# Infini-attention plus SiLU MLP on one core: k's first masked tile read from PSUM by two engines, the exponentials' table loaded ahead of the last v copy, the first tile of x in two halves, and a newly searched order of pieces

## The chip, the core and the metric

The kernel runs on one core of a Trainium2 chip. The metric is the device time of one execution in microseconds (us), the median of three runs. Engines are named as in the profile: PE is TensorE (matmuls), PEld its weight loads, DVE is VectorE, ACT is ScalarE, POOL is GpSimd, SP is SyncE, which here only issues DMAs (a q behind an engine's name means its DMA issues).

## The reference, cut to what matters

```
xn = layernorm(A_x)                       # 2048 rows of 512, bf16
q, k, v = xn @ wq, xn @ wk, xn @ wv       # 32 heads of 16, 4 segments of 512 rows
for s in 4 segments:
    p     = softmax(qs ks^T * 16**-0.5 + mask)      # within the segment
    a_dot = p @ vs
    a_mem = (phi(qs) @ M) / (phi(qs) . z + 1e-6)    # phi(t) = t+1 if t > 0 else exp(t)
    o     = g * a_mem + (1 - g) * a_dot             # g = sigmoid(beta), by head
    M += phi(ks)^T @ vs;  z += sum phi(ks)
out = A_x + o @ wo + silu(xn @ w1) @ w2             # w1 512 x 1792, w2 1792 x 512
```

The mask is added where the key's row lies behind the query's (`ar[:, None] < ar[None, :]`), so attention is causal within a segment.

## The kernel before, in words

All tensors are tiled to 128 partitions. x has 16 tiles of 128 rows; a segment is four of them. Four heads of k or q lie in 64 partitions, so one tile of kT or qT (128 partitions x 512 rows of a segment) holds eight heads, and a segment has four such tiles.

No scheduler orders the work. A string, ORDER, lists 1333 pieces by name, and the kernel issues them in that order (`tc.manual_schedule()`); each engine gets its instructions in the order of the list and waits, in place, for what an instruction needs. So the list is the queue of every engine at once. A piece's name holds its kind, its segment and its place. The ones that matter here:

- `xc`, `xd` (together `xs`): mean and variance of one tile of x on VectorE. `xq`, `xi`: square root on ScalarE, reciprocal on VectorE, for the first four tiles; `xg`: the same on GpSimd for four later tiles at once. `Nv`: the normalised tile. `X` with `Xa` or `Xv`: its transposes by TensorE and the copy to xnT by ScalarE or VectorE; `XD`: a DMA transpose, for the later tiles.
- `v`, `k`, `q`, `h`: parts of the products of xnT with wv, wk, wq, w1. In segments 0 and 1 a part is a quarter of a tile, in segments 2 and 3 a half. In segment 0, parts 0 and 1 of k, q and h cover the first 256 rows, parts 2 and 3 the others. `va` and `vv`, `qa` and `qv`, `ka` and `kv` copy the finished tile from PSUM, on ScalarE or on VectorE; `ha` is the tanh of a tile of h, `hv` the rest of its SiLU.
- `ka`/`kv` call `k_copy`: one copy of the tile to kT, and then two copies by GpSimd from kT to k3, with every odd or every even head set to zero (`pm_odd`, `pm_even`, which the piece `odd` makes). The score products need them, because a row group of TensorE spans two heads.
- `fp`, `fa`, `fv`: phi of k, its positive part on GpSimd, its exponential on ScalarE, the sum on VectorE (`gp`, `ga`, `gv` for q).
- `S` and a number: one score block. TensorE fills psS, a tile of four PSUM banks of which there is one, and ScalarE takes the exponential of all 2048 elements of a partition (line 707). There are 72. GpSimd then sets the masked corners to zero (line 718), in place and into a second tile, lows. `E` and `O` weigh v with them (line 763), for the even and the odd heads; `Ev`, `Ea`, `Ov`, `Oa` copy the result.
- `o`, `oc`, `od`, `oh`: whole, half, quarter and half-width products of the output; `st`, `sh` store. `n`, `z`, `d`, `r`, `R`, `w`, `W`, `s`: the memory's part and the softmax's division.
- `tb`: one small exponential on ScalarE, `first_exp` (line 304), in front of which the build puts the load of the table with exp and tanh. The square roots ahead of it use another table, which the small square root on line 185 loads.
- `busy`: products of zeros on TensorE, which fill its time before x is there.
- `kind`, `odd`, `omask`, `ones`, `zeros`: constants.

TensorE has three tilings: whole, four strips of columns (`cols`) and four of rows (`rows`, for scores). A dense product is issued whole or as four strips, by what stands before and behind it in the list.

The loads at the start: tiles 0 and 2 of x, then wv in halves, wk, wq, and the rest are issued by SyncE, tiles 1 and 3 by ScalarE (line 158 and on). The DMAs use eight semaphores in turn, so a ninth waits, in its issuing queue, until the one eight places ahead has landed. PSUM has four single banks for everything else than psS.

## Time and profile before

| what | value |
|---|---|
| median of three runs (lowest to highest) | 222.32 us (222.01 to 222.53) |
| profiled execution | 222.15 us |
| its span in the profile | 220.4 us |
| PE busy | 214.9 us, 97% |
| ACT busy | 184.0 us, 83% |
| DVE busy | 179.7 us, 82% |
| POOL busy | 135.1 us, 61% |
| granted TensorE clock, mean | 0.999 |

The span runs from the first to the last instruction of the profile; 1.75 us of the execution lie around it. Busy shares are means over a start, a long middle part and an end, whose limits differ. In the rows of the timeline stand start (us from the span's start), length (us), engine, line, operation, output and inputs, count, and in brackets the idle time before it with the releaser. Rows of several instructions are merged. In the rows by stretch stand, for each engine in the order PE, PEld, DVE, ACT, POOL, the busy time and the number of instructions, then the granted clock, the busy share of the DMA engines and GB/s.

### The profile page before, as it was taken

The page shows a single profiled execution, that of the slowest core. Times are in us where ns is not written, and L with a number is a line of the kernel's source. Part 1 is how long each engine was busy: PE and PEld are TensorE (multiplying, and loading weights), DVE is VectorE, ACT ScalarE, POOL GpSimd, SP SyncE. Part 2 cuts the span into 40 slices and gives each one's busy share as a digit, 9 for nine tenths or more (in the row PEclk, how much of TensorE's full clock was granted, in tenths as well). Part 3 has the DMA queues.
Part 4 walks back from the last instruction along what each step waited for, and adds up shares of the span by engine and source line. Part 5 has one row for each costly group of instructions (what it writes and reads, how often), then busy time and mean ns, then how long its engine had stood idle before and what let it go on. Part 6 is the DMA issues. An engine that isn't in the chain of part 4 may idle for free.

```text
span 220.4 us, 9441 instructions
## 1 busy us (share of the span) xinstructions
PE 214.9 (97%) x4057; PEld 117.2 (53%) x4057; DVE 179.7 (82%) x368; ACT 184.0 (83%) x173; POOL 135.1 (61%) x253
## 2 busy tenths in 40 slices
PE   7999999999999999999999999999999999999994
PEld 7666645655553444454544444455454544455662
DVE  7789999988889788776897888969789887579554
ACT  3699999999999999999998999999989997971000
POOL 6089667997769976876669696693756364320000
PEclk9999999999999999999999999999999999999999
DMA  5993549552014221223303130142242020232313
GB/s 183 373 385 87 74 27 304 106 77 58 21 28 122 88 59 29 50 51 76 102 17 95 40 96 4 28 92 59 52 120 64 15 76 7 75 94 68 109 51 97
DMA packets 32746, 19.61 MB, mean 89 GB/s; under 512 B 14656, under 2 KB 32192, under 8 KB 32704
## 3 DMA queue, kind: packets, MB, share of 16 engines
q1 hardware_dynamic: 30080, 16.39, 28.6%
q10 hardware_dynamic: 2624, 2.62, 3.9%
q8 instruction: 31, 0.51, 1.0%
q14 instruction: 11, 0.09, 0.2%
HBM read 9.96 MB, written 2.10 MB: 55 GB/s over the span
## 4 chain that ended last, share of the span: by engine, by line
PE 79%; ACT 10%; DVE 4%; POOL 4%; issue 2%; POOLq 0%
PE ps L331 21%; PE psO L333 16%; PE ps L333 13%; PE psS L701 10%; PE psO L331 9%; ACT Pb L707 7%; PE psV L763 6%; PE psS L333 4%; POOL Pb L718 2%; DVE xn_t L310 1%; POOL lows L718 1%; ACT ex L408 1%; ACT th L477 1%; PE psM L437 1%; DVE stats L281 1%
## 5 line engine op out<-in xcount | busy, mean ns | idle before, releaser
L707 ACT ACTIVATE Pb<-psS 128x2048 bf16<-128x2048 f32 x72 | 135.2, 1878 | 7.5 <-PE psS L701 6.4
L718 POOL TENSOR_SCALAR_AFFINE_SELECT Pb<-Pb 128x256 bf16<-128x256 bf16 (+2 forms) x120 | 66.1, 571 | 22.3 <-ACT Pb L707 19.5
L482 DVE SCALAR_TENSOR_TENSOR hT<-th,ps 128x512 bf16<-128x512 bf16 x56 | 37.7, 679 | 9.1 <-ACT th L477 8.5
L718 POOL TENSOR_SCALAR_AFFINE_SELECT lows<-Pb 64x256 bf16<-64x256 bf16 (+1 forms) x56 | 26.7, 490 | 27.7 <-ACT Pb L707 25.3
L333 PE MATMUL psO<-w_sb,hT 128*32 128x512 bf16 (+2 forms) x716 | 42.5, 319 | 0.0
L331 PE MATMUL ps<-xnT,w_sb 128*128 128x512 bf16 (+1 forms) x160 | 35.2, 334 | 0.0
L477 ACT ACTIVATE th<-ps 128x512 bf16<-128x512 f32 x56 | 33.0, 598 | 2.2 <-PE ps L333 2.1
L333 PEld LDWEIGHTS <-hT 128*32 128x32 bf16 x884 | 21.8, 96 | 14.0 <-issue 3.3
L333 PE MATMUL ps<-xnT,w_sb 128*32 128x512 bf16 (+1 forms) x480 | 27.1, 341 | 0.1
L701 PE MATMUL psS<-qT,k 32*128 32x64 bf16 (+3 forms) x512 | 23.0, 233 | 0.8 <-ACT Pb L707 0.3
L331 PE MATMUL psO<-w_sb,hT 128*128 128x512 bf16 (+2 forms) x87 | 22.7, 334 | 0.0
L701 PEld LDWEIGHTS <-k 32*128 32x128 bf16 x512 | 9.8, 92 | 23.2 <-issue 21.7
L763 PE MATMUL psV<-Pb,Vz 128*32 128x448 bf16 (+7 forms) x512 | 21.6, 286 | 0.3 <-POOL Pb L718 0.3
L331 PEld LDWEIGHTS <-w_sb 128*128 128x128 bf16 x160 | 14.9, 98 | 12.1 <-issue 1.6
L763 PEld LDWEIGHTS <-Vz 128*32 128x32 bf16 x768 | 16.5, 97 | 9.1 <-issue 1.1
L376 POOL TENSOR_SCALAR k<-kT,pm_odd 128x512 bf16<-128x512 bf16 x16 | 12.0, 748 | 8.0 <-ACT kT L373 7.0
L333 PEld LDWEIGHTS <-w_sb 128*32 128x32 bf16 x480 | 11.9, 96 | 7.3 <-issue 1.9
L331 PE MATMUL ps<-wv_sb,xnT 128*128 128x512 bf16 x56 | 15.1, 381 | 0.2
L701 PE MATMUL psS<-qT,kT 16*128 16x448 bf16 (+3 forms) x256 | 14.7, 269 | 0.0
L333 PE MATMUL psO<-wo_sb,oT 128*32 128x512 bf16 x156 | 14.4, 380 | 0.0
L331 PE MATMUL ps<-xnT,wk_sb 128*128 128x256 bf16 (+1 forms) x64 | 13.6, 326 | 0.0
L793 DVE CAST oraw<-psV 128x512 bf16<-128x512 f32 x16 | 11.0, 689 | 3.0 <-PE psV L763 2.9
(110 smaller groups left out, 321.2 us busy)
## 6 DMA issues: line engine op xcount, KB each, us to landing
spr<-rz SPq DMA_DIRECT2D x56, 64.0 KB
x_res<-in_A_x_dram SPq DMA_DIRECT2D x16, 128.0 KB
out_dram<-o_out SPq DMA_DIRECT2D x15, 128.0 KB
w_sb<-in_B_w_dram SPq DMA_DIRECT2D x1, 1792.0 KB
w_sb<-in_B_w_dram ACTq DMA_DIRECT2D x1, 1792.0 KB
x_hi<-in_A_x_dram SPq DMA_DIRECT2D x2, 512.0 KB
wv_sb<-in_A_wv_dram SPq DMA_DIRECT2D x2, 256.0 KB
wk_sb<-in_A_wk_dram SPq DMA_DIRECT2D x1, 512.0 KB
```

The costliest lines, as they stand in the source:

```text
L281: nc.vector.bn_stats(out=stats[t][:], in_=xs(t, t + 1)[:, 0, :])
L310: eng.tensor_scalar(out=xn[t][:], in0=xs(t, t + 1)[:, 0, :], scalar1=mv_all[:, t, 0:1], scalar2=rstd_all[:, t, 0:1], op0=ALU.subtract, op1 ...
L331: return [nc.tensor.matmul(out, lhsT=lhsT, rhs=rhs, start=start, stop=stop, skip_group_check=True)]
L333: nc.tensor.matmul(out[c : c + 32], lhsT=lhsT[:, c : c + 32], rhs=rhs, start=start, stop=stop, tile_position=(0, c), skip_group_check=True,)
L376: nc.gpsimd.tensor_scalar(out=to, in0=frm, scalar1=keep[:, 0:1], scalar2=1.0, op0=ALU.mult, op1=ALU.mult)
L477: nc.scalar.activation(out=th[:], in_=sts[s]["h", ft][:, :], func=AF.Tanh, scale=0.5)
L482: nc.vector.scalar_tensor_tensor(out=st["hT"][:, ft, :], in0=st.pop(("th", ft))[:], scalar=1.0, in1=st.pop(("h", ft))[:, :], op0=ALU.add, ...
L701: nc.tensor.matmul(psS[:, g, c : c + q2 - q1], lhsT=keys[rows], rhs=st["qT"][rows, dt, q1:q2], start=True, stop=True, tile_position=(32 * ...
L707: exp = nc.scalar.activation(out=Pb[:, :, :], in_=psS[:, :, :], func=AF.Exp, scale=SCALE)
L718: over[id(Pb)].append(nc.gpsimd.affine_select(out=out, in_=in_, compare_op=ALU.is_ge, fill=0.0, base=base, pattern=[[0, out.shape[1]], [1, ...
L763: nc.tensor.matmul(psV[32 * g : 32 * g + 32, q0 : q0 + nq], lhsT=Vzs[s % 2][:, kt, 4 * dt + g, par : par + 2, :].rearrange("p a d -> p (a ...
L793: copy(out=oraw[:], in_=sts[s].pop(("psV", 0))[:, :])
```

## The change

Tile 0 of x is loaded as two halves of 64 rows, one from each of the two queues; tiles 1, 2 and 3 follow on the same queues as before. A new piece, `kf`, is used for the first tile of k of segment 0: ScalarE copies the tile from PSUM to kT, VectorE makes the odd heads' masked copy straight from PSUM and ScalarE the even heads'. All other tiles of k are made as before. In the list, `tb` stands between the two v copies `va0.0` and `va0.1`, three pieces of constants stand later than the first statistics, the first `busy` has 40 products, and the pieces behind are in another order (of which the first lines are shown). The number of score blocks and of products is the same, but for the 40 products of zeros.

```diff
-kind odd omask ones0 ones1 zeros xc0 xd0 xc1 xq0 xi0 Nv0 busy44 xd1 xq1 xc2 xi1 X0.1 Nv1 xd2 Xa0.1 busy6 v0.0.0 v0.0.1 xq2 X1.1 Xa1.1 xs3 v0.0.2 v0.0.3 xq3 v0.1.0 xi2 v0.1.1 v0.1.2 v0.1.3 Nv2 xi3 X2.1 va0.0 va0.1 Nv3 Xv2.1 X3.1 Xv3.1 k0.0.0 k0.0.1 k0.1.0 k0.0.2 k0.0.3 k0.3.0 q0.0.0 q0.0.1 q0.0.2 q0.0.3 ka0.0 fp0.0 qv0.0 tb fa0.0 q0.2.0 k0.1.1 k0.1.2 k0.1.3 kv0.1 fp0.1
-S0 q0.1.0 q0.1.1 q0.1.2 q0.1.3 k0.3.1 xs4 xs6 xs7 xs5 xg4.4 q0.2.1 q0.2.2 qa0.1 q0.2.3 qv0.2
-S2 v0.2.0 v0.2.1 k0.3.2 k0.3.3 kv0.3 fa0.1 v0.3.0 v0.3.1 v0.3.2 Nv7 v0.2.2 XD7 v0.2.3
-S1 Nv5 vv0.2 h0.5.0 h0.10.0 h0.10.1 h0.10.2 v0.3.3 vv0.3 xs8 Nv6 XD6 h0.5.1 h0.5.2 XD5 h0.5.3 ha0.5
-S3 q0.3.0 q0.3.1 q0.3.2 q0.3.3 hv0.5 k0.2.0 qv0.3 Nv4 XD4 k0.2.1 k0.2.2 tanh h0.10.3 ha0.10
-S4 fv0.0 k0.2.3 kv0.2 h0.11.0 h0.11.1 h0.11.2 h0.11.3 ha0.11 fv0.1 v1.3.0 v1.3.1 v1.3.2 v1.3.3
-S7 vv1.3 hv0.10 h0.13.0 h0.13.1 fa0.3 h0.13.2 hv0.11 fp0.2 O0 E0 Ev0 Ov0
-S5 v1.2.0 v1.2.1 v1.2.2 h0.13.3 ha0.13 v1.2.3 xs9 vv1.2 q1.1.0 q1.1.1 q1.1.2 q1.1.3 qv1.1 xs11
-S11 Om0 v1.0.0 hv0.13 v1.1.0 v1.0.1 v1.0.2 v1.1.1 v1.0.3 h0.1.0 h0.1.1 h0.1.2 fp0.3 ga1.1
...
+ones0 ones1 zeros xc0 xd0 xc1 xq0 xi0 Nv0 busy40 xd1 xq1 xc2 xi1 X0.1 Nv1 xd2 Xa0.1 busy6 v0.0.0 v0.0.1 xq2 X1.1 Xa1.1 xs3 v0.0.2 v0.0.3 xq3 v0.1.0 xi2 v0.1.1 v0.1.2 v0.1.3 Nv2 va0.0 xi3 tb Nv3 X2.1 Xv2.1 X3.1 k0.0.0 k0.0.1 k0.1.0 Xv3.1 k0.0.2 k0.0.3 q0.0.0 q0.0.1 va0.1 odd kf0.0 xs6 q0.0.2 q0.0.3 qa0.0 xs4 k0.1.1 k0.1.2 k0.1.3 ka0.1
+S0 fa0.1 q0.1.0 q0.1.1 k0.3.0 q0.1.2 q0.1.3 xs5 qv0.1 xs7 q0.2.0 q0.2.1 q0.2.2 q0.2.3 qv0.2 xg4.4
+S2 k0.2.0 k0.2.1 k0.2.2 k0.2.3 v0.2.0 v0.2.1 k0.3.1 kv0.2 Nv5 XD5 fp0.1 k0.3.2 k0.3.3 Nv6 fa0.0
+S1 v0.2.2 h0.11.0 h0.11.1 h0.11.2 h0.11.3 ha0.11 v0.2.3 kv0.3 q0.3.0 q0.3.1 h0.13.0
+S3 h0.13.1 vv0.2 fv0.1 XD6 h0.13.2 h0.13.3 ha0.13 Nv7 q0.3.2 q0.3.3 qv0.3 v0.3.0 v0.3.1 v0.3.2 hv0.11 v0.3.3 vv0.3 XD7
+S4 h0.5.0 h0.5.1 h0.5.2 h0.5.3 ha0.5 v1.2.0 v1.2.1 v1.2.2 Nv4 fp0.0 hv0.13 v1.1.0 v1.1.1 XD4 xs9 fp0.2 hv0.5
+S7 h0.10.0 v1.1.2 v1.1.3 vv1.1 h0.10.1 h0.10.2 E0 v1.2.3 xs8 Ev0 fa0.2
+S5 h0.1.0 h0.1.1 h0.10.3 ha0.10 fv0.0 h0.1.2 h0.1.3 fp0.3 vv1.2 k1.2.0 k1.2.1 k1.2.2 k1.2.3
+S11 fv0.2 kv1.2 fp1.2 v1.0.0 v1.0.1 v1.0.2 v1.0.3 ha0.1 hv0.10 h0.7.0 h0.7.1 h0.7.2 vv1.0 h0.7.3 xs10 O0 Ov0 fa0.3
...
@@ -154,16 +154,18 @@
     wo_sb = cpool.tile([P, DT, D], BF16, name="wo_sb")
     beta_r = cpool.tile([P, 1], BF16, name="beta_r")
 
-    def load_x(eng, t0, n):
+    def load_x(eng, t0, n, rows=slice(0, P)):
         eng.dma_start(
-            out=xs(t0, t0 + n),
-            in_=x_flat[t0 * P : (t0 + n) * P, :].rearrange("(n p) d -> p n d", p=P),
-        )
-
-    load_x(nc.sync, 0, 1)
+            out=xs(t0, t0 + n)[rows],
+            in_=x_flat[t0 * P : (t0 + n) * P, :].rearrange("(n p) d -> p n d", p=P)[rows],
+        )
+
+    load_x(nc.sync, 0, 1, slice(0, P // 2))
+    load_x(nc.scalar, 0, 1, slice(P // 2, P))
     load_x(nc.scalar, 1, 1)
     load_x(nc.sync, 2, 1)
     load_x(nc.scalar, 3, 1)
+
     def load_w(eng, w_sb, W, k0, k1):
         eng.dma_start(out=w_sb[:, k0:k1, :], in_=W.rearrange("(ko ki) n -> ki ko n", ki=P)[:, k0:k1, :])
 
@@ -367,15 +369,28 @@
 
 
 
-    def k_copy(s, dt, copy=nc.vector.tensor_copy):
+    def k_tiles(s, dt):
         kT = seg_tile(s, "kT")
         k3 = sts[s]["k3", dt] = segp.tile([P, TPS, 3 * HP], BF16, name="k3", bufs=6)
-        copy(out=kT[:, dt, :], in_=sts[s].pop(("k", dt))[:, :])
-        k_in = kT[:, dt, :].rearrange("p (t c) -> p t c", c=P)
-        for to, frm, keep in ((k3[:, :, HP : 3 * HP], k_in, pm_odd), (k3[:, :, 0:HP], k_in[:, :, 0:HP], pm_even)):
+        return kT[:, dt, :], (k3[:, :, HP : 3 * HP], k3[:, :, 0:HP])
+
+    def k_copy(s, dt, copy=nc.vector.tensor_copy):
+        kT, (odd, even) = k_tiles(s, dt)
+        copy(out=kT, in_=sts[s].pop(("k", dt))[:, :])
+        k_in = kT.rearrange("p (t c) -> p t c", c=P)
+        for to, frm, keep in ((odd, k_in, pm_odd), (even, k_in[:, :, 0:HP], pm_even)):
             nc.gpsimd.tensor_scalar(
                 out=to, in0=frm, scalar1=keep[:, 0:1], scalar2=1.0, op0=ALU.mult, op1=ALU.mult
             )
+
+    def k_fast(s, dt):
+
+        kT, (odd, even) = k_tiles(s, dt)
+        ps = sts[s].pop(("k", dt))
+        k_in = ps[:, :].rearrange("p (t c) -> p t c", c=P)
+        nc.scalar.copy(out=kT, in_=ps[:, :])
+        nc.vector.tensor_scalar(out=odd, in0=k_in, scalar1=pm_odd[:, 0:1], scalar2=None, op0=ALU.mult)
+        nc.scalar.activation(out=even, in_=k_in[:, :, 0:HP], func=AF.Copy, scale=pm_even[:, 0:1])
 
     def q_mm(s, dt, part):
         dense(s, "q", wq_sb, dt, part)
@@ -841,7 +856,7 @@
         "E": lambda n: weigh(n, 0), "Ev": lambda n: even_copy(n, vec), "Ea": lambda n: even_copy(n, act),
         "Om": odd_merge, "omask": make_omask,
         "O": lambda n: weigh(n, 1), "Ov": lambda n: odd_copy(n, vec), "Oa": lambda n: odd_copy(n, act),
-        "k": k_mm, "kv": k_copy, "ka": lambda s, dt: k_copy(s, dt, act),
+        "k": k_mm, "kf": k_fast, "kv": k_copy, "ka": lambda s, dt: k_copy(s, dt, act),
         "q": q_mm, "qv": q_copy, "qa": lambda s, dt: q_copy(s, dt, act),
         "v": v_mm, "vv": v_copy, "va": lambda s, j: v_copy(s, j, act),
         "h": h_mm, "ha": h_tanh, "hv": h_silu,
```

128 lines of the change are left out of this document (64 added, 64 removed).

## The prediction

> **What bounds the kernel now.** I read the page first (busy times, the chain that ended last), then the busy time by stretch of the run, then the timeline of the first 20 us.
>
> ```profile
> span 220.4 us, 9441 instructions
> PE 214.9 (97%) x4057; PEld 117.2 (53%) x4057; DVE 179.7 (82%) x368; ACT 184.0 (83%) x173; POOL 135.1 (61%) x253
> ...
> PE 79%; ACT 10%; DVE 4%; POOL 4%; issue 2%; POOLq 0%
> ```
>
> ```profile
> 15.00:20.00 5.00, 4.83 (x58) 2.89 (x57) 4.67 (x11) 4.97 (x5) 4.44 (x10) 1.00 0.61 188
> 100.00:120.00 20.00, 20.00 (x385) 9.57 (x387) 16.44 (x35) 18.93 (x16) 14.04 (x25) 1.00 0.26 69
> ```
>
> TensorE (PE) is busy for 214.9 of 220.4 us and is 79% of the chain; between 100 and 120 us it is never idle. ScalarE (ACT) is full early (4.97 of 5 us), and at 100 to 120 us it has a little room (18.93 of 20). So a change gains only by giving TensorE products sooner at the start, or by closing small gaps between its products. "Busy" hides those gaps, because the ends of matmuls are modelled; they show in the distance between the starts of two score blocks:
>
> ```profile
> 15.04 0.40 PE L701 MATMUL psS<-qT,k 32*128 32x64 bf16 x8 [0.28 <-ACT Pb L707]
> ...
> 15.37 0.60 PE L331 MATMUL ps<-wv_sb,xnT 128*128 128x512 bf16 x2
> 15.48 1.88 ACT L707 ACTIVATE Pb<-psS 128x2048 bf16<-128x2048 f32 x1
> 15.81 0.60 PE L331 MATMUL ps<-xnT,wk_sb 128*128 128x256 bf16 x4
> 16.25 1.24 PE L331 MATMUL ps<-wv_sb,xnT 128*128 128x512 bf16 x5
> 17.42 0.21 PE L701 MATMUL psS<-qT,k 32*128 32x64 bf16 x4
> 17.76 1.05 PE L331 MATMUL ps<-xnT,w_sb 128*128 128x256 bf16 x8
> 18.65 0.38 PE L331 MATMUL ps<-wv_sb,xnT 128*128 128x512 bf16 x1
> 18.86 0.82 PE L331 MATMUL ps<-xnT,w_sb 128*128 128x256 bf16 x6
> 19.81 0.40 PE L701 MATMUL psS<-qT,k 32*128 32x192 bf16 x8
> ```
>
> The prices of a product and of a weighting's piece are in the chain, in order of time:
>
> ```profile
> 88.07 0.86 PE ps L331 x4
> ...
> 114.57 0.54 PE psV L763 x16
> ```
>
> A score block fills the one buffer psS, its exponential takes 1.88, and the next block can't start before that has read psS; with one short ScalarE instruction between two exponentials the blocks come every 17.42 - 15.04 = 2.38 us. The first row of the chain prices a product of 512 columns at 0.86/4 = 0.215 (two of 256 are the same). I call that one part: it is one piece k, q, v or h of segments 0 and 1. Between 15.04 and 17.42 stand 2 + 2 + 5 = 9 parts, 1.94, and scores with both changes of tiling take the other 0.44: the block is full. Between 17.42 and 19.81 stand 4 + 1 + 3 = 8 parts: the same 2.39 us hold 0.22 of nothing. Such gaps are what a list can still win.
>
> **The start, step by step.**
>
> ```profile
> 1.40 1.23 DVE L257 MEMSET lows<- 64x1408 uint32 x1 [0.35 <-issue]
> ...
> 3.65 0.70 DVE L281 BATCH_NORM_STATS2 stats<-x_lo 128x6 f32<-128x512 bf16 x1
> ```
>
> ```profile
> 2.00:3.00 1.00, 1.00 (x13) 1.00 (x11) 0.94 (x4) 0.99 (x1) 1.00 (x3) 1.00 0.66 226
> 3.00:4.00 1.00, 1.00 (x12) 1.00 (x11) 0.96 (x8) 0.20 (x1) 1.00 (x3) 1.00 0.99 338
> ```
>
> Tile 0 of x is needed at 3.65. Today VectorE works on constants until then (lows to 2.63, then kind to omask), so its arrival can't be read off; moving the constants alone gains nothing if the tile arrives near 3.6. In halves on both queues it no longer shares the engines with tile 1: 226 GB/s bring tiles 0 and 1 (256 KB) by about 3.1, tile 0 alone by about 2.6, so up to 0.5 earlier, and 0 if the queue of ScalarE is the later one. I take 0.35, nearer to the transfer's own sum. Tiles 1 and 3 come somewhat later; they are wanted 0.8 and over 3 us behind tile 0. The warm-up on zraw is 40 products instead of 44 and ends earlier, as the first transposes come earlier. The SyncE queue now has wq waiting for tile 0's half before it is issued; the DMA engines are full then (0.99 from 3 to 4), so its bytes queue anyway, and its first product comes behind k's, after 10; nothing.
>
> ```profile
> 8.16 0.58 ACT L391 CAST Vz<-ps 128x512 bf16<-128x512 f32 x1
> ...
> 9.16 0.76 DVE L823 COPY xnT<-ptr 128x512 bf16<-128x512 bf16 x2 [0.24 <-PE ptr L817]
> 10.60 0.59 ACT L373 CAST kT<-ps 128x512 bf16<-128x512 f32 x1 [1.08 <-PE ps L331]
> 11.20 1.28 ACT L304 ACT_TABLE_LOAD   x1
> 11.29 0.70 POOL L376 TENSOR_SCALAR k<-kT,pm_odd 128x512 bf16<-128x512 bf16 x1 [7.01 <-ACT kT L373]
> 11.69 0.69 DVE L384 CAST qT<-ps 128x512 bf16<-128x512 f32 x1 [1.78 <-PE ps L331]
> 11.97 0.48 POOL L376 TENSOR_SCALAR k<-kT,pm_even 128x256 bf16<-128x256 bf16 x1
> 12.51 0.21 PE L701 MATMUL psS<-qT,k 32*128 32x64 bf16 x4
> 12.61 0.61 ACT L408 ACTIVATE ex<-kT 128x512 bf16<-128x512 bf16 x1
> 13.13 1.86 ACT L707 ACTIVATE Pb<-psS 128x2048 bf16<-128x2048 f32 x1
> ```
>
> ```profile
> L823 ACT COPY xnT<-ptr 128x256 bf16<-128x256 bf16 x4 | 1.3, 375 | 0.3 <-PE ptr L817 0.2
> ```
>
> From 3.65 to 9.92 (9.16 + 0.76) the path is VectorE's, in the same order in both lists, so all of it moves by 0.35: the last xnT copy ends at 9.57, and k's first tile, which ended just before 10.60, is there at 10.25. ScalarE: the first v copy starts at 7.81 (8.16 - 0.35), ends at 8.39; now the table load follows; the next copy can start 1.41 behind it (11.20 to 12.61 today, the small exponential between), so the second v copy runs 9.8 to 10.4, and kT starts at about 10.3: the load, 1.4 with its exponential off the path from kT to the first scores, costs at most 0.1 in front of kT. It does leave the path: today it stands between kT and the first exponential.
>
> Now the masked copies. As the changed kernel is built, VectorE's copy (odd) waits for ScalarE's kT, and ScalarE's masked copy (even) waits for VectorE's: the three readers of this one PSUM tile go one after the other. kT 10.3 to 10.9; semaphore 0.1 (11.19 to 11.29 today); odd at the price of a VectorE copy from PSUM, 0.69, to 11.7; even about 0.4 (256 elements, the last row: 375 ns), to 12.15. Today's GpSimd copies take 0.70 + 0.48: only 0.1 is saved. And qT, which VectorE made beside them (11.69), now stands behind them on ScalarE: 0.59, to 12.7. First scores at 12.8 instead of 12.51; kT of tile 1 stands ahead of the first exponential (to 13.25), so that starts at 13.3 instead of 13.13, and the second score block at 15.2 instead of 15.04.
>
> By then TensorE has done 29 parts (8 v, 9 k, 12 q) instead of 30 (8 v, 10 k, 12 q), 0.22 more to do later. Start: +0.16 + 0.22 = +0.38. Bounds: -0.6 if nothing is serial, +0.75 if the halves gain nothing.
>
> The rule that bears on this is in the Trainium skill, PSUM — Partial Sum Buffer, section "PSUM bank collisions raise a hardware error": two engines may not read one bank at the same time, so their reads must be ordered. That speaks against this part; no run here shows a collision, and the sum by it is the serial one above, while copies side by side give the first rival below. Nothing else here needs that sentence: the waits are in the program.
>
> **The list behind it.** The pieces are the same ones, but for k's first tile (one masked copy each goes from GpSimd to VectorE and ScalarE) and one more kT that ScalarE copies in VectorE's place; changes between tilings stay at 144. I counted TensorE's work in each of the 71 stretches between score blocks in both lists (parts by 0.215, the pieces E and O of a weighting at 0.54, 0.43 for scores and changes) and added up what is missing to 2.38. Before: 2.2 us in all, 1.1 of it in the first twelve stretches, where six hold 8 parts. After: 1.2 us, 0.2 in the first twelve (nine parts in nearly all), 0.7 in the next twelve (0.6 before), 0.3 behind (0.5). Without the first stretch, which the start already counts, 2.0 becomes 1.2: -0.78. Between the first and the last block ScalarE has two copies fewer and one exponential of k more than today, so it does not take this back; GpSimd does more in the first four stretches (masked copies of three tiles of k instead of two, 0.70 + 0.48 each). I take -0.78 in full, with 0 (every gap filled by another wait) to -1.1 as bounds.
>
> **The end.** Behind the last score block stand 23.5 us of products instead of 24.2 (the same count of pieces by prices), so what is done more before it is not done there. The last piece is still a half store, and oT's last part is first multiplied 3.6 us ahead of the end: 0 (0.2 either way).
>
> Sum: 222.15 (the profiled execution; span 220.4 and 1.75 around it) + 0.38 - 0.78 = 221.75. The median of the runs is 222.32, 0.17 more; so **221.9**.
>
> **Rivals.**
>
> *Copies side by side.* If the three readers did run beside each other, even would end at 11.3, qT at 11.8, the first exponential would start at 12.3 and the second score block at 14.25: 0.95 less, 220.9. Against it: the waits as built. Chance 0.09.
>
> *The list gives nothing.* The gaps in the sum are a count of work, not of waits; today's kernel has waits that such a count doesn't see, as the one in the first row here; the next two are prices for the rival behind:
>
> ```profile
> PE psV L763 <- POOL Pb L718: 0.3, 1, 0.3
> ```
>
> ```profile
> L718 POOL TENSOR_SCALAR_AFFINE_SELECT Pb<-Pb 128x1024 bf16<-128x1024 bf16 x8 | 8.7, 1093 | 0.5
> L718 POOL TENSOR_SCALAR_AFFINE_SELECT lows<-Pb 64x512 bf16<-64x512 bf16 x8 | 6.2, 773 | 4.9 <-ACT Pb L707 4.6
> ```
>
> If new ones fill the gaps, -0.78 goes and 222.7 is left. Chance 0.14, half of it over the bound below.
>
> *GpSimd late (slower).* In the new list E0, the first weighting, stands ahead of O0, behind five parts of its stretch, at 26.3; it needs the masks of the fifth exponential (ends about 24.7), which take 0.77 + 1.09: 26.55 if GpSimd is free. Ahead of them stand the two masked copies of k's fourth tile (0.70 + 0.48). If those copies are still to do at 24.7, TensorE waits 1.2 at E0, and the buffers of the exponentials with it: 223.1. It decides if GpSimd is over 0.3 behind at 24.7; below that the wait is about 0.25, inside the range. That first row speaks against (one wait of 0.3 for a mask in the whole run). Chance 0.17.
>
> *The table load costs more in its new place.* Today the load starts 0.01 behind the end of kT (10.60 + 0.59). If in the new place ScalarE first had to run empty for as long again (1.28), kT and all behind it would be that much later: 223.2. Chance 0.04. The Trainium skill, ScalarE: Activation LUTs, section "What ACT_TABLE_LOAD costs", gives a drain of 1.38 besides the load of 1.283; by it the sum would be 223.3. The trace agrees on the load (1.28) and shows no drain.
>
> **How the numbers follow.** About 0.2% (0.44 us) is what a measurement of this kernel can tell from no change: below 221.88 is faster, over 222.76 slower. The likeliest case (0.56) lies on the lower bound with some 0.4 either way: 0.28 faster, 0.27 same, 0.01 slower. Side by side 0.09 faster; the empty list 0.08 same, 0.06 slower; GpSimd 0.17 and table 0.04 slower. Together 0.37 faster, 0.35 same, 0.28 slower. Range: 221.2 to 223.0, which leaves out the side-by-side case, the table and a third of the GpSimd case; the likeliest case alone spans 221.5 to 222.4.
>
> **What would show it.** First statistics at about 3.3; kT on ScalarE at 10.3 with VectorE's masked copy starting only when it ends; first scores at 12.8, second at 15.2; the next score blocks 2.38 to 2.40 apart with nine parts each; E0 at about 26.3. Wrong: first scores below 12.0 (side by side), a wait for GpSimd at E0 over 0.5, or stretches of 2.6 with nine parts.

## The result and the profile after

The changed kernel took 224.83 us (median of six executions, 223.50 to 225.48) against 222.16 us (221.99 to 222.53) for the kernel before: 1.0114 times as long, 95% interval 1.0081 to 1.0147. The forecast was 221.9, with a range to 223.0. Measured once more beside the experiments it took 223.96 (223.16 to 225.05) against 222.39, ratio 1.0066 (1.0043 to 1.0089): slower again, by less, and with a wide spread. The execution in the profile is one of the two slowest (225.48; span 223.8). Medians, ranges and ratios in this document leave out executions over 1.5% above the fastest of the same kernel, of which there is one (e4_side, 227.01 us).

The page of the changed kernel (span, busy times, shares of the chain):

```profile
span 223.8 us, 9535 instructions
PE 215.2 (96%) x4098; PEld 116.9 (52%) x4098; DVE 179.1 (80%) x368; ACT 185.5 (83%) x175; POOL 133.6 (60%) x251
...
PE 78%; POOL 7%; ACT 5%; DMA 4%; DVE 2%; issue 2%; SPq 1%; POOLq 0%; DVEq 0%
```

TensorE's busy time rose by 0.3 us, the span by 3.4. DMA, which had no share in the chain before, now has 4%. The timeline of the start shows one place of it (start, length, engine, line, operation; SPq is SyncE's issuing):

```profile
0.79 1.45 SPq L158 DMA_DIRECT2D x_lo<-in_A_x_dram  x2
2.28 0.94 SPq L170 DMA_DIRECT2D wv_sb<-in_A_wv_dram  x2
3.42 0.69 DVE L283 BATCH_NORM_STATS2 stats<-x_lo 128x6 f32<-128x512 bf16 x1 [0.78 <-DMA x_lo<-in_A_x_dram]
8.28 0.17 DVE L303 RECIPROCAL rstd_all<-rstd_all 128x1 f32<-128x1 f32 x1 [0.31 <-ACT rstd_all L300]
8.74 1.28 ACT L306 ACT_TABLE_LOAD   x1
9.13 0.76 DVE L838 COPY xnT<-ptr 128x512 bf16<-128x512 bf16 x2 [0.24 <-PE ptr L832]
10.13 1.26 PE L333 MATMUL ps<-xnT,wk_sb 128*128 128x256 bf16 x10 [0.78 <-DMA wk_sb<-in_A_wk_dram]
11.43 0.59 ACT L391 CAST kT<-ps 128x512 bf16<-128x512 f32 x1 [0.72 <-PE ps L333]
12.05 0.75 DVE L392 TENSOR_SCALAR k<-ps,pm_odd 128x512 bf16<-128x512 f32 x1 [2.04 <-ACT kT L391]
12.84 0.47 ACT L393 ACTIVATE k<-ps,pm_even 128x256 bf16<-128x256 f32 x1 [0.82 <-DVE k L392]
13.21 0.58 ACT L399 CAST qT<-ps 128x512 bf16<-128x512 f32 x1
13.84 0.21 PE L716 MATMUL psS<-qT,k 32*128 32x64 bf16 x4 [0.49 <-ACT qT L399]
16.25 0.40 PE L716 MATMUL psS<-qT,k 32*128 32x64 bf16 x8
```

TensorE waits for wk until 10.13, so first scores and second score block stand at 13.84 and 16.25 (before 12.51 and 15.04). That is the worst of the starts seen: in the second measurement's profile they stand at 12.98 and 15.38. Another place is the end, here first of the kernel before, then of the changed one (VectorE's timeline; o_out is a whole output, o_half half of one):

```profile
214.25 0.42 DVE L653 SCALAR_TENSOR_TENSOR o_half<-psS,x_res 128x256 bf16<-128x256 f32 x1 [2.24 <-PE psS L333]
214.69 0.69 DVE L606 SCALAR_TENSOR_TENSOR o_out<-psO,x_res 128x512 bf16<-128x512 f32 x1
216.09 0.69 DVE L606 SCALAR_TENSOR_TENSOR o_out<-psO,x_res 128x512 bf16<-128x512 f32 x1 [0.71 <-PE psO L333]
216.75 0.69 DVE L606 SCALAR_TENSOR_TENSOR o_out<-psS,x_res 128x512 bf16<-128x512 f32 x1
217.61 0.42 DVE L653 SCALAR_TENSOR_TENSOR o_half<-psS,x_res 128x256 bf16<-128x256 f32 x1 [0.17 <-PE psS L333]
```

```profile
216.57 0.69 DVE L621 SCALAR_TENSOR_TENSOR o_out<-psS,x_res 128x512 bf16<-128x512 f32 x1 [2.29 <-PE psS L335]
217.50 0.69 DVE L621 SCALAR_TENSOR_TENSOR o_out<-psO,x_res 128x512 bf16<-128x512 f32 x1 [0.23 <-PE psO L335]
218.36 0.69 DVE L621 SCALAR_TENSOR_TENSOR o_out<-psO,x_res 128x512 bf16<-128x512 f32 x1 [0.17 <-PE psO L335]
220.34 0.76 DVE L668 SCALAR_TENSOR_TENSOR o_half<-psS,x_res 128x256 bf16<-128x256 f32 x2 [1.29 <-DMA out_dram<-o_out]
```

Before, one half output is made 3.4 us ahead of the other and only that one is left for the end. In the new list three whole outputs stand first and both halves behind them. They share three buffers (`o_half` has the tag of `o_out`), so the first half waits for the transfer of an output that was issued at 217.29. From the start of TensorE's last product (217.3 before, 219.2 after) to the end of the span it is 3.1 us before and 4.5 after. Start (1.2 us) and end (1.4) leave about 0.7 us to the part between them, to which the last part of this text comes back.

### The profile page after: what moved, and what is told of

The parts are those of the page before. It is cut to its first block, busy times and chain, and to the rows that moved or that the text cites. A ratio compares the mean times of both kernels' runs of the same rounds, so it can differ in the third digit from the quotient of the medians.

```text
span 223.8 us, 9535 instructions
## 1 busy us (share of the span) xinstructions
PE 215.2 (96%) x4098; PEld 116.9 (52%) x4098; DVE 179.1 (80%) x368; ACT 185.5 (83%) x175; POOL 133.6 (60%) x251
## 4 chain that ended last, share of the span: by engine, by line
PE 78%; POOL 7%; ACT 5%; DMA 4%; DVE 2%; issue 2%; SPq 1%; POOLq 0%; DVEq 0%
PE ps L333 17%; PE ps L335 16%; PE psO L335 14%; PE psO L333 10%; PE psS L716 9%; PE psV L778 7%; ACT Pb L722 3%; DMA wk_sb<-in_A_wk_dram 3%; POOL Pb L733 3%; PE psS L335 3%; POOL k L382 2%; POOL lows L733 1%; DMA out_dram<-o_out 1%; SPq L158 1%; PE psM L452 1%
## 5 line engine op out<-in xcount | busy, mean ns | idle before, releaser
L733 POOL TENSOR_SCALAR_AFFINE_SELECT Pb<-Pb 128x256 bf16<-128x256 bf16 (+2 forms) x120 | 68.0, 587 | 19.9 <-ACT Pb L722 15.9
L335 PE MATMUL psO<-w_sb,hT 128*32 128x512 bf16 (+2 forms) x664 | 41.5, 323 | 0.0
L333 PE MATMUL ps<-xnT,w_sb 128*128 128x512 bf16 (+1 forms) x154 | 31.5, 330 | 0.6 <-DVE odd L815 0.6
L335 PE MATMUL ps<-xnT,w_sb 128*32 128x512 bf16 (+1 forms) x504 | 30.3, 346 | 0.3 <-issue 0.3
L335 PEld LDWEIGHTS <-hT 128*32 128x32 bf16 x832 | 20.3, 96 | 14.7 <-issue 3.4
L333 PE MATMUL psO<-w_sb,hT 128*128 128x512 bf16 (+2 forms) x100 | 24.2, 326 | 0.0
L382 POOL TENSOR_SCALAR k<-kT,pm_odd 128x512 bf16<-128x512 bf16 x15 | 10.8, 720 | 12.3 <-ACT kT L379 10.1
L335 PEld LDWEIGHTS <-w_sb 128*32 128x32 bf16 x504 | 12.8, 96 | 9.3 <-issue 2.3
L333 PEld LDWEIGHTS <-hT 128*128 128x128 bf16 x100 | 9.1, 98 | 9.4 <-issue 1.3
L808 DVE CAST oraw<-psV 128x512 bf16<-128x512 f32 x14 | 9.6, 686 | 4.7 <-PE psV L778 4.7
L335 PE MATMUL psO<-wo_sb,oT 128*32 128x512 bf16 x144 | 13.3, 380 | 0.0
```

The costliest lines, as they stand in the source:

```text
L333: return [nc.tensor.matmul(out, lhsT=lhsT, rhs=rhs, start=start, stop=stop, skip_group_check=True)]
L335: nc.tensor.matmul(out[c : c + 32], lhsT=lhsT[:, c : c + 32], rhs=rhs, start=start, stop=stop, tile_position=(0, c), skip_group_check=True,)
L382: nc.gpsimd.tensor_scalar(out=to, in0=frm, scalar1=keep[:, 0:1], scalar2=1.0, op0=ALU.mult, op1=ALU.mult)
L733: over[id(Pb)].append(nc.gpsimd.affine_select(out=out, in_=in_, compare_op=ALU.is_ge, fill=0.0, base=base, pattern=[[0, out.shape[1]], [1, ...
L808: copy(out=oraw[:], in_=sts[s].pop(("psV", 0))[:, :])
```

## The experiments

Eighteen runs were made, in five groups; those of a group shared a chip and the executions of the kernel before. The table gives them in the order of the text. The ratios are not those of the two medians beside them: where single executions are long the two differ, most for h3_halves (medians 0.51 us apart, ratio 1.07 us).

| run | what it is | median (range), us | before beside it | ratio, 95% interval |
|---|---|---|---|---|
| e1_whole | changed, tile 0 whole | 223.43 (223.41 to 224.02) | 222.45 | 1.0054 (1.0041 to 1.0067) |
| e2_halves | before, tile 0 in halves | 222.65 (222.37 to 224.50) | 222.45 | 1.0023 (1.0006 to 1.0039) |
| e3_halfbuf | changed, own buffers for halves of outputs | 223.20 (222.17 to 225.40) | 222.45 | 1.0044 (1.0022 to 1.0065) |
| e4_side | changed, first k masked from kT | 223.46 (222.90 to 224.50) | 222.45 | 1.0052 (1.0033 to 1.0072) |
| f1_end | e1, end of the list mended | 223.66 (223.00 to 224.85) | 222.36 | 1.0054 (1.0031 to 1.0077) |
| f2_endside | f1, first k masked from kT | 222.93 (222.29 to 223.34) | 222.36 | 1.0013 (0.9995 to 1.0031) |
| f3_oldlist | e1's start, the old list behind it | 223.11 (222.83 to 223.44) | 222.36 | 1.0022 (1.0008 to 1.0036) |
| f4_esh | f2, tile 0 in halves | 223.26 (222.58 to 224.37) | 222.36 | 1.0036 (1.0018 to 1.0054) |
| g1_all | f2, own buffers | 221.71 (221.27 to 222.44) | 222.39 | 0.9971 (0.9957 to 0.9984) |
| g2_after | the changed kernel again | 223.96 (223.16 to 225.05) | 222.39 | 1.0066 (1.0043 to 1.0089) |
| g3_end2 | f1, own buffers | 222.41 (222.04 to 223.06) | 222.39 | 1.0003 (0.9990 to 1.0016) |
| g4_oldside | f3, first k masked from kT | 222.12 (221.85 to 223.30) | 222.39 | 0.9983 (0.9967 to 1.0000) |
| h1_merged | g3, halves, tiles 2 and 3 in one transfer | 223.56 (222.58 to 224.65) | 222.28 | 1.0059 (1.0037 to 1.0082) |
| h2_third | g3, tile 3 in halves instead | 222.91 (222.72 to 223.55) | 222.28 | 1.0038 (1.0024 to 1.0052) |
| h3_halves | g3, tile 0 in halves | 222.79 (222.43 to 225.36) | 222.28 | 1.0048 (1.0024 to 1.0072) |
| h4_kv | g1, one copy of k later | 222.97 (221.81 to 223.62) | 222.28 | 1.0022 (1.0006 to 1.0038) |
| i1_wide | g1, eleven products whole | 221.82 (220.94 to 222.60) | 222.07 | 0.9982 (0.9964 to 0.9999) |
| i2_g1 | g1 again | 221.80 (221.31 to 222.33) | 222.07 | 0.9977 (0.9963 to 0.9992) |

My theory after the first look: the halves make the weights late, and the end waits for buffers. The rivals: the weights are late for another reason; the end is one execution's accident.

**e1_whole**

```diff
-    load_x(nc.sync, 0, 1, slice(0, P // 2))
-    load_x(nc.scalar, 0, 1, slice(P // 2, P))
+    load_x(nc.sync, 0, 1)
```

> The changed kernel with tile 0 of x loaded whole, in one transfer on SyncE's queue, as before; all else is the changed kernel. In the changed kernel's trace the first product of wk waits for its weights until 10.13 us (9.97 before, without that wait) and the first of wq until 11.64, the first scores stand at 13.84 and the second score block at 16.25. Theory: the halves delay the transfers behind them (the first two issues of SyncE took 1.45 us instead of 0.87, and one of the sixteen parts of wk landed 1.3 us behind the others). Then, whole, wk's and wq's products no longer wait, first scores come at 12.8, the second block at 15.2, and the median falls from 224.8 by about 1.0 to 223.8. Rival A: the weights are late for another reason (the constants' and the table load's new places): second block stays near 16.2, median 224.8. Rival B: the start is slack for the rest of the run and other waits take it back: second block 15.2, median over 224.4.

SyncE's first two issues take 0.87 us again, wk's first product stands at 9.23, and the second score block at 15.46, not 15.2. The last product starts at 217.32, within 0.03 us of the kernel before; all the time that is left over lies behind it (rows of the end):

```profile
214.66 0.69 DVE L620 SCALAR_TENSOR_TENSOR o_out<-psS,x_res 128x512 bf16<-128x512 f32 x1 [2.29 <-PE psS L334]
215.58 0.69 DVE L620 SCALAR_TENSOR_TENSOR o_out<-psO,x_res 128x512 bf16<-128x512 f32 x1 [0.23 <-PE psO L334]
216.45 0.69 DVE L620 SCALAR_TENSOR_TENSOR o_out<-psO,x_res 128x512 bf16<-128x512 f32 x1 [0.17 <-PE psO L334]
218.33 0.76 DVE L667 SCALAR_TENSOR_TENSOR o_half<-psS,x_res 128x256 bf16<-128x256 f32 x2 [1.19 <-DMA out_dram<-o_out]
```

So the start with the serial copies and the new list together cost TensorE nothing here, and the wait for a buffer is there in an execution of another kernel too. Not an accident, then.

**e2_halves**: the two lines the other way, in the kernel before.

> The kernel before with one thing changed: tile 0 of x in two halves of 64 rows on the two queues. VectorE's constants and the list stay. Theory (the halves delay the weights behind them): the weights' issues come 0.6 us later, k's first product waits, the second score block moves from 15.04 to between 15.4 and 16.2, median 222.6 to 223.4, with more spread from run to run than the 0.5 us of the kernel before. Rival: the halves cost nothing by themselves; median 222.2, second block 15.0.

The second block moved to 15.22 only; the median rose by 0.20 us, at the lower edge, the highest execution by 1.7. SyncE's two issues take 1.46 us here too.

**e3_halfbuf**

```diff
-        o_half = work.tile([P, D], BF16, name="o_half", tag="o_out", bufs=3)[:, 0 : D // 2]
+        o_half = work.tile([P, D], BF16, name="o_half", tag="spr", bufs=4)[:, 0 : D // 2]
```

> The changed kernel with the last two half outputs (o_half) in buffers of their own kind (those of spr, free by then) instead of the three that they share with o_out. In the changed kernel's trace VectorE waits 1.29 us before the half outputs, for the transfer of a whole output issued at 217.3 us to land, and both half outputs are made only at 220.34, though TensorE's last product starts at 219.23. Theory: three whole outputs and two halves stand within 3 us at the end of the new list, with three buffers; the halves are then made at about 219.2 and 219.6, the end comes 0.7 us earlier, median 224.1. Rival: the wait is that one run's own (one of sixteen parts of that transfer landed 1.2 us behind the others); in most runs the buffer is free in time, median 224.7 to 224.8.

The wait is gone: the halves are made at 216.82 and 217.37, around the start of the last product (217.04).

```profile
216.82 0.97 DVE L668 SCALAR_TENSOR_TENSOR o_half<-psS,x_res 128x256 bf16<-128x256 f32 x2
217.94 0.88 SPq L672 DMA_DIRECT2D out_dram<-o_half  x2
```

The end is shorter, but not that of the kernel before: 3.9 us from the start of the last product, since SyncE issues the five outputs one behind the other and comes to the first half, made by 217.24, only at 217.94. The median is 0.75 us above the kernel before; the changed kernel later measured 1.57 above it, on another chip. In this profile the weights came in time in spite of the halves (second block 15.29, 0.09 from the forecast): what the halves do changes from execution to execution.

**e4_side** (k_sb is kT in the shape of k_in)

```diff
-        nc.vector.tensor_scalar(out=odd, in0=k_in, scalar1=pm_odd[:, 0:1], scalar2=None, op0=ALU.mult)
-        nc.scalar.activation(out=even, in_=k_in[:, :, 0:HP], func=AF.Copy, scale=pm_even[:, 0:1])
+        nc.vector.tensor_scalar(out=odd, in0=k_sb, scalar1=pm_odd[:, 0:1], scalar2=None, op0=ALU.mult)
+        nc.gpsimd.tensor_scalar(out=even, in0=k_sb[:, :, 0:HP], scalar1=pm_even[:, 0:1], scalar2=1.0, op0=ALU.mult, op1=ALU.mult)
```

> The changed kernel with other masked copies of k's first tile: ScalarE copies PSUM to kT as now, then VectorE makes the odd heads' copy from kT, not from PSUM, and GpSimd the even heads' copy from kT beside it; ScalarE makes none. In the changed kernel's trace kT ends at 12.02, odd at 12.80, even at 13.31, qT at 13.79, first scores at 13.84: one after the other. Theory (the three readers of one PSUM tile in a row set the first scores): odd and even end at about 12.6, qT, whose products end at 12.7, at 13.3, first scores at 13.35, 0.5 us earlier, median 224.3. Rival: the first scores are set by q's late weights, or what is gained is taken back by waits in the list behind: median 224.7 to 224.9.

From the start of kT to the first scores it is 1.48 us (11.23 to 12.71) instead of 2.41. In the time this can't be told from the changed kernel, since that kernel was not beside it; the pairs f1 and f2, f3 and g4, g3 and g1 price it below.

**f1_end**

```diff
-... zv3.3 nv3.3 oh17.0 oc3.0.3.0 ... oh9.0 ... st3.1 oh1.0 oh14.0 oh0.0 oh2.0 oh5.0 oh16.0 sh0 oh13.1 ...
+... zv3.3 nv3.3 oh9.0 oh1.0 oh14.0 oh0.0 oh2.0 oh5.0 oh16.0 oh17.0 sh0 oc3.0.3.0 ... st3.1 oh13.1 ...
```

> The changed kernel with tile 0 whole (as in the run above) and, at the end of the list, the seven last products of the first half output and its store (sh0) moved ahead of the stores of tiles 2, 0 and 1 of the last segment; as in the kernel before, one half output is then left for the end. Buffers as in the changed kernel. With tile 0 whole alone TensorE's last product starts at 217.32, as in the kernel before (217.29), but the span ends 1.19 us later (221.62 against 220.43): the halves are made at 218.33 and 218.67. Theory (five outputs in a row, behind three buffers and one queue, are what the end costs): last half made within 0.3 us of the last product, span 220.5, median 223.4 - 1.1 = 222.3. Rival: the products moved ahead push the whole outputs back by as much as they free, and the end stays over 4 us behind the last product: median 223.2 or more.

A miss: the time did not fall. VectorE's rows show why:

```profile
214.83 0.42 DVE L667 SCALAR_TENSOR_TENSOR o_half<-psS,x_res 128x256 bf16<-128x256 f32 x1 [2.52 <-PE psS L334]
215.37 0.69 DVE L620 SCALAR_TENSOR_TENSOR o_out<-psS,x_res 128x512 bf16<-128x512 f32 x1
216.18 0.69 DVE L620 SCALAR_TENSOR_TENSOR o_out<-psO,x_res 128x512 bf16<-128x512 f32 x1
217.98 0.69 DVE L620 SCALAR_TENSOR_TENSOR o_out<-psO,x_res 128x512 bf16<-128x512 f32 x1 [1.10 <-DMA out_dram<-o_half]
```

The wait moved to the third whole output, which is now the fourth in three buffers. Outputs so close together wait in both orders tried; before, the fourth output came 2.5 us behind the first. The Trainium skill, DMA: Bandwidth & Descriptors, section "Anatomy of one DMA — SWDGE (gpsimd) path", has a fixed 2.0 us per transfer, most of it the receipt of the write, for another path than the one used here. The trace has a time of that size for SyncE's: the half output issued at 215.28 frees its buffer just ahead of 217.98, 2.7 us later.

**f2_endside** is f1_end with e4_side's edit.

> The kernel with tile 0 whole and the end of the list mended, and besides the first tile of k masked from kT: VectorE makes the odd copy and GpSimd the even one, side by side, ScalarE none. With tile 0 whole, q's first tile is multiplied by 11.49 us and kT ends at 11.23; the first scores come at 13.05 and the second score block at 15.46. Theory (the chain of three readers of one PSUM tile, then qT on the same engine, sets the first scores): first scores at 12.2 (11.5 + 0.6 for qT), second block at 14.6, median 222.3 - 0.8 = 221.5, below the kernel before. Rival: the 0.8 us earlier are lost again within the first 50 us, where masks and copies wait; median 222.1 or more.

The first scores came at 11.90 and the second block at 14.33, and the last product started at 216.33, 0.94 us ahead of f1's: what the start gained was kept to the last product. The buffer wait (1.05 us) is still there; median 0.73 us below f1. The forecast of 221.5 is missed by 1.4, because the end that it took as mended was not.

**f3_oldlist**: e1_whole with `k0.3.0 q0.2.0 fp0.0 fa0.0 fp0.1` again ahead of S0 and the old lines from S0 on.

> The changed kernel's code and start (tile 0 whole, the serial copies of k's first tile, the table load between the two v copies) with the list of the kernel before from the first score block on, its end included. The part of k and the part of q that the old list has done by then (k0.3.0, q0.2.0) stand in the start again, as do both feature copies, and qT is ScalarE's. Theory (the new list's closer order is worth 0.8 us before 130 us and loses 0.4 by a wait at 148; the start costs some 0.4): first scores at 13.0, second block at 15.4, end 220.8, median 222.8. Rival (the new list gives nothing): the stalls behind 20 us sum to the same as with the new list, median 222.3, the same as with the mended end.

It took 0.75 us more than the kernel before, with the old end: the changed start in front of the old list is a loss. The first scores came at 13.38, later than forecast, for a reason that I had not seen:

```profile
12.42 0.38 PE L332 MATMUL ps<-xnT,wq_sb 128*128 128x256 bf16 x2 [0.74 <-ACT k L392]
```

The three readers in a row also hold one of the four PSUM banks until the last has read. The profiles with the new list don't have this wait, so it belongs to this pairing of start and list.

**f4_esh** is f2_endside with the halves.

> The kernel with the mended end and the masked copies from kT, but with tile 0 of x in halves, as in the changed kernel. Against the same kernel with tile 0 whole this is the price of the halves. Theory (the halves cost 0.6 us of issue on SyncE and let single parts of the weights fall behind by up to 1.3 us, from run to run): median 0.2 to 0.8 above the kernel with tile 0 whole and over 1 us between lowest and highest, where the whole tile has under 0.7. Rival (the halves bring tile 0 about 0.1 us sooner and cost nothing): median 0.1 to 0.2 lower and no wider spread.

0.33 us more than f2, and 1.8 us between lowest and highest (f2: 1.05).

**g1_all** is f2_endside, **g3_end2** is f1_end, each with e3_halfbuf's edit; **g2_after** is the changed kernel; **g4_oldside** is f3_oldlist with e4_side's edit.

> Tile 0 whole, the masked copies of k's first tile from kT, the end of the list mended, and the two half outputs in buffers of their own (those of spr). With the first three alone VectorE's last whole output waited 1.05 us for the first half output's transfer, since both kinds share three buffers, and the span ended 4.2 us behind the start of the last product (3.1 in the kernel before). Theory (what the end costs is the wait for a buffer): no such wait, the last half made at 216.9, end within 3.3 us of the last product, 1.0 us off the run without it: median 221.9. Rival (the outputs' transfers themselves are in a row, and the buffer wait only hides that): end still 4 us behind the last product, median 222.7 or more.

> The changed kernel once more, unchanged, beside the others on the same chip, to price the parts against it. Theory (start late by the halves in some executions, five outputs in a row at the end): median 224.0 to 224.8 with over 1 us between lowest and highest; against the kernel with only tile 0 whole (0.5 to 0.6% above the kernel before on its chip) 0.3 to 1.0 us more. Rival (its first measurement was that chip's own): median within 0.2 us of 223.4.

> The changed kernel with tile 0 whole, the end of the list mended and the half outputs in buffers of their own; the first tile of k is masked as in the changed kernel (three readers in a row). It leaves the change's start and its list and takes away both the halves and the end. Theory: the second score block comes at 15.45 (0.4 late), the list wins that back by the last product (217.3 in both kernels), and the end is that of the kernel before: median 222.4, the same as before. Rival (the end is the transfers themselves): median 223.4 or more.

> The list of the kernel before behind the changed start, as in the earlier run, but with the first tile of k masked from kT, side by side on VectorE and GpSimd. In the earlier run the first scores came at 13.38: ScalarE's even copy held the PSUM tile until 12.36, and a product of q waited 0.74 us for that bank. Theory: first scores at 12.3, second block at 14.8, 1.0 us earlier, median 222.1 to 222.3; against the kernel with the new list, the mended end and the same start this is what the new list is worth, 0.3 to 0.6 us. Rival (the start's gain is lost behind, in waits of the old list): median 222.8 or more.

This group settles the sizes, on one chip. g3 has the change's serial copies and its list, without the halves and without the shared buffers: 222.41 against 222.39. The forecast was 222.4, but so close by luck: in the profile the second block (15.29) and the last product (217.02) come 0.2 and 0.3 sooner than forecast, and the end is 0.3 longer. The halves and the end together therefore are the changed kernel's loss on this chip (1.55 of 1.57 us). g1 against g3: the serial copies cost 0.70. g1 against g4: the new list is worth 0.41 with the quick start; g3 against f3, each by its kernel before: 0.73 with the serial one. g1 is 0.29% faster than the kernel before. Its end shows no wait:

```profile
216.56 0.69 DVE L622 SCALAR_TENSOR_TENSOR o_out<-psO,x_res 128x512 bf16<-128x512 f32 x1 [0.17 <-PE psO L334]
217.17 0.41 DVE L669 SCALAR_TENSOR_TENSOR o_half<-psS,x_res 128x256 bf16<-128x256 f32 x1
```

**h1_merged, h2_third, h3_halves**: g3_end2 with other transfers of x.

```diff
 h3: load_x(nc.sync, 0, 1, slice(0, P // 2)); load_x(nc.scalar, 0, 1, slice(P // 2, P)); the rest as it was
 h1: the same halves; load_x(nc.scalar, 1, 1); load_x(nc.sync, 2, 2)
 h2: tile 0 whole; load_x(nc.scalar, 3, 1, slice(0, P // 2)); load_x(nc.scalar, 3, 1, slice(P // 2, P))
```

> The kernel with the changed start and list, the mended end and own buffers for the half outputs (222.41 with tile 0 whole, on its chip as long as the kernel before), with tile 0 in halves of 64 rows on the two queues, but tiles 2 and 3 in one transfer on SyncE, so that four transfers bring x, as in the kernel before. Theory A (a transfer of 64 rows is dearer to issue than one of 128): SyncE's first two issues take well over 0.87 us and wv's issue starts at about 2.2, median 0.3 to 0.6 above the kernel before. Theory B (the fifth transfer is what costs, by its issue and by moving every later transfer to the next of the eight semaphores): with four transfers the price goes; median within 0.2 us of the kernel before.

> The same base with tile 0 whole, but tile 3 of x in two halves of 64 rows, both issued by ScalarE, so five transfers bring x. No half stands in SyncE's queue. Theory A (the 64-row issue ahead of the weights): SyncE's first two issues take about 0.87 us again and the weights come as with the whole tile; median within 0.2 us of the kernel before. Theory B (a fifth transfer shifts the semaphores of all later ones, and waits between 43 and 49 us grow from 0.9 to 1.4): median 0.3 to 0.6 above the kernel before and a spread of over 1 us.

> The same base with tile 0 in halves exactly as in the changed kernel (five transfers, one half on each queue): the price of the halves on a kernel whose end is that of the kernel before. Theory: wv's issue starts at 2.28 instead of 1.70, median 0.3 to 0.6 us above the kernel before, with over 1 us between lowest and highest. Rival: the halves cost nothing once the end is mended (it was the end that turned their disturbance into time): median within 0.2 us of the kernel before.

h3 prices the halves: 0.51 us by the medians, 1.07 by the ratio (0.5 to 1.6). In its profile, one of its quick executions, the second block stands at 15.49 (g3: 15.29) and the span ends 0.26 later; of its long executions, up to 225.36, there is no profile here. Neither theory explains it alone. In h1, with four transfers, SyncE's first two issues still take 1.45 us; so the price of the issue is the halves', not the fifth transfer's. One issue of 64 rows took 0.55 to 0.60 us in the eight profiles with tile 0 in halves, and the 128 rows behind it on SyncE 0.81; without halves 128 rows took 0.39 to 0.47. But h2, whose SyncE issues the first two in 0.87 again, loses as well (0.63), though nothing of 64 rows stands ahead of the weights. That h1 is the slowest has a plain part: tile 2 comes with tile 3 in one transfer ahead of the weights, and TensorE waits 0.65 us for wv. In h2's profile TensorE waits for wv too (0.22 and 0.19) and the second block stands at 15.54, 0.25 behind g3's; what the rest of its loss comes from is open.

**h4_kv**

```diff
-S42 dv1.3 k3.0.1 fv2.1 fa2.0 kv3.0 xl1.0 ...
-S39 h1.7.0 ...
+S42 dv1.3 k3.0.1 fv2.1 fa2.0 xl1.0 ...
+S39 kv3.0 h1.7.0 ...
```

> The fastest kernel so far (tile 0 whole, masks of the first k from kT, mended end, own buffers: 221.71, 0.3% below the kernel before) with one piece moved in its list: the copy kv3.0 with its two masked copies on GpSimd stands at the start of the next score block's stretch. In all kernels with the new list TensorE waits 0.36 us at the weighting E9 (at 148.76 in the changed kernel), since those two copies (0.69 + 0.72) stand on GpSimd ahead of the masks that E9 needs. Theory: the wait goes, and with TensorE full from there to the end the median falls by 0.3 to 221.4. Rival: the copy's PSUM bank is held longer, or the wait comes back one stretch later; median 221.6 to 221.9.

A miss, and my error: kv3.0 stands near 120 us. The masked copies ahead of the weighting at 148 are another tile's, and the wait there is unchanged. Near 120 us the moved copy has the effect that the rival named: its PSUM tile is held until 121.13 (until 117.25 in i2, the same list without the move), and a product waits. Counted product by product, that costs 0.6 us against i2. It is not the whole loss: the median is 0.69 above the kernel before, and g1's was 0.69 below. Another 0.9 us stands in this profile before 50 us, in gaps like the one that follows.

```profile
120.58 1.05 PE L334 MATMUL ps<-wv_sb,xnT 128*32 128x512 bf16 x16 [0.35 <-DVE hT L498]
```

**i1_wide, i2_g1**

```diff
-S10 h0.8.0 t0.3 ...
+S10 wide h0.8.0 t0.3 ...      ("wide" sets the tiling of what follows to whole)
```

> The fastest kernel so far (tile 0 whole, masks of the first k from kT, mended end, own buffers) with one thing changed: the eleven products of the stretch behind S10, which the list runs as four strips each because a weighting stands behind them, run whole, which is 33 matmuls and 33 weight loads fewer and one change of tiling more. In many traces of the new list TensorE has a gap of 0.6 to 0.95 us, each time ahead of the same instruction (number 1219 of its stream in the changed kernel, first product behind S13), and it ends 1.2 to 1.6 us behind the end of a transfer of 16 KB of the queue that the page calls instruction; 32 of these make 0.52 MB, which is TensorE's 8209 instructions at 64 bytes. Just ahead of the gap it goes through 154 instructions within some 2 us. Theory (TensorE there runs out of instructions; how long it waits depends on how soon the transfer gets through): with 66 instructions fewer ahead of it the gap goes, waits from 40 to 50 us sum to 0.8 or less in the profile, the spread narrows to under 0.8 us, and the median is 0 to 0.3 below the same kernel beside it (0.1 of it paid for the change of tiling). Rival (the gap is a wait for a copy or a transposing transfer): the gap stays, and the median is 0.1 above.

> The fastest kernel so far once more, unchanged, beside the run above on the same chip. Both theories: median 221.5 to 222.0, 0.2 to 0.4% below the kernel before, with 1 us or more between lowest and highest.

Undecided. The gap that these two ask about is, in the second profile of the changed kernel, this one:

```profile
44.07 0.83 PE L333 MATMUL ps<-xnT,w_sb 128*128 128x256 bf16 x6 [0.70 <-DVE odd L815]
```

It stands in 11 of the 16 profiles with the new list, 0.56 to 0.94 us from one start to the next, and in none of the four with the old one. The row names a copy, odd, as what ended the wait; it was not, as two other profiles show. In h2_third the same product starts before that copy has ended, and in h4_kv the gap stands one product earlier, ahead of a score product for which no release is seen:

```profile
43.40 0.68 DVE L815 CAST odd<-psV 128x512 bf16<-128x512 f32 x1
44.04 0.83 PE L333 MATMUL ps<-xnT,w_sb 128*128 128x256 bf16 x6 [0.55 <-DVE qT L399]
```

```profile
43.49 0.24 PE L717 MATMUL psS<-qT,kT 16*128 16x192 bf16 x1 [0.59 <-issue]
```

In i1 the gap is absent, and TensorE is idle for 0.06 us from 40 to 50; but the control's profile doesn't have the gap either (0.28 idle; 0.32 in the kernel before). i1's last product started 0.8 us sooner, its end took 0.7 longer (last half issued at 217.49), and the medians are equal. The spread did not narrow. i2 confirms g1: 221.80 against 222.07, 0.23% faster.

## Why the prediction was wrong, point by point

**The end (the step that failed most).** The prediction looked at the last piece, "still a half store", and wrote 0. It did not look at what stands ahead: five outputs within 3 us for three buffers. Runs: e1 is 0.98 us above the kernel before with the wait, g3 0.02 without. So about 1.0 us. It takes both remedies: from the start of the last product to the end of the span it is 4.3 us in e1, 4.3 with the order alone mended (f1), 3.9 with the buffers alone (e3), 3.5 with both (g3), and 3.1 in the kernel before.

**The halves (failed in sign).** Taken as 0.35 sooner, with "nothing" for the queues. The first statistics did come 0.23 sooner (3.42), but hardly by the halves: with tile 0 whole and the constants later they stand at 3.45 in g3 (3.14 to 3.62 in eleven profiles). And the last transposed copy came only 0.03 sooner (9.13): VectorE waited 0.31 for ScalarE on the way, a wait that "all of it moves by 0.35" had left out. In place of a gain the halves cost 0.51 us (h3). What the traces show of it are issues of weights that start 0.58 later (2.28 against 1.70 for wv) and, in some executions, one of sixteen parts of a weight far behind the rest (in the first profile wk's last part landed 1.3 us behind the last but one). I had summed the bytes and not the issuing. That these two are all of the cost is not shown, since h2 loses without a half in front of the weights.

**The serial copies (right).** kT, odd, even, qT one after the other, as read from the waits: 11.43, 12.05, 12.84, 13.21. odd took 0.75 (taken 0.69), even 0.47 (0.4). With weights in time (second profile) first scores stand at 12.98 and the second block at 15.38, forecast 12.8 and 15.2. That they are so near is in part luck: the forecast has 0.35 from the halves in it, and g3, without them, has 12.89 and 15.29. (The prediction's own sum has the second v copy end at 10.38, so kT at 10.4, not 10.3.) The rival "side by side" was out, yet side by side was to be had from kT: 0.7 us.

**The table load (right).** Off the path, 8.74 to 10.02. The first v copy (8.14, 0.59) ended 0.01 ahead of it: no drain in this place either, so that rival is out.

**The list (right in kind, not safe).** Forecast -0.78; the runs give -0.41 (g4 to g1, 95% interval about -0.1 to -0.7) and -0.73 (f3 to g3; f3 has the wait for a bank in it, so this is rather too much). The cadence is as forecast (16.25, 18.64, 21.05, 23.44 in the first profile). Waits that a count of work doesn't see took a part: 0.36 us at the weighting at 148 in every profile with this list, and the gap near 44. By stage, one profile each (us):

| profile | second block at | from there to the last product | from there to the end |
|---|---|---|---|
| before | 15.04 | 202.25 | 3.14 |
| forecast | 15.2 | 201.7 | 3.1 |
| g3 | 15.29 | 201.73 | 3.46 |
| h3 (g3 with the halves) | 15.49 | 201.77 | 3.47 |
| changed, first profile | 16.25 | 202.99 | 4.53 |
| changed, second profile | 15.38 | 202.46 | 4.91 |

In g3 and h3 the middle is what the forecast has (202.25 + 0.22 - 0.78). In the changed kernel's own two profiles nothing of the list's gain is left: the gap near 44 us is 0.85 and 0.94 from start to start, and the first profile has another, 0.64, at 48.77. So the list's term failed in these executions by waits, and why they are longer in some executions than in others stays open.

**GpSimd late (out).** The first weighting stands 11.0 us behind the second score block, as forecast (11.1), and waits about 0.3 for masks, not 1.2.

**The number.** The start at +0.38 and the list at -0.78 sum to -0.40, and the start has the halves' gain of 0.35 in it. Without that gain the serial copies and the list give -0.05; measured for those two, g3: 0.02. The changed kernel beside it is at +1.57. The end (1.0 instead of 0) and the halves (+0.5 instead of -0.35) are nearly all of the 1.97 between. The bounds allowed the halves to gain nothing and the end 0.2; no case had either of them cost more.

## What to carry to other kernels

When a list is searched anew, compare its last few microseconds with the old one's: how many outputs follow each other within the time that one transfer needs to free its buffer, how many buffers there are, and how long the queue that issues them is busy. Two halves of a transfer on two queues are not half the price: count the issues that stand ahead of the next load, and measure. The engines that read one PSUM tile went one behind the other here and held the bank; try to let one copy it to SBUF and the others work from there.

## What I had not expected of the hardware

An issue of 64 rows was dearer than one of 128 (0.55 to 0.60 us against 0.39 to 0.47), and SyncE's next one took 0.81. The Trainium skill, Perfetto Trace Analysis, section "DMA Instruction — HWDGE (DVE, Sync)", says that the profiled span of such an instruction contains a wait for the exclusive use of the generator of descriptors; no run here separates that wait from the work.

VectorE's masked copy took 0.35 us from kT in SBUF (bf16, g1) and 0.75 from PSUM (f32, the changed kernel).

The profile has a queue named instruction, which carries pieces of 16 KB. Their sum, if it is TensorE's alone, comes to 64 bytes for each of its 4098 + 4098 instructions:

```profile
q8 instruction: 32, 0.52, 1.0%
```

In the 11 profiles with the gap near 44 us TensorE goes on 1.2 to 1.7 us behind the end of such a piece, wherever between 42.7 and 44.8 us that is, and no wait of the program accounts for it. That points to TensorE running out of instructions. But pieces may themselves be fetched as TensorE goes on, and then the two would move together in any case; no run here proves it, and why the new list's executions spread over 1 us stays open.
